# Dealing the products with the values in two stretches per unit

## The chip, the cores and the metric

One core of one Trainium2 chip runs the whole kernel. The metric is the device time of one execution in microseconds (us); the median of three executions of the kernel before is 1018.26 us.

## The reference, cut to what matters

The input `x` has 2048 tokens (rows) of 512 values. A vector `c` gives six modulation rows (shift, scale and gate for each of two blocks). The first block is sliding-window attention with 32 heads of 16 dimensions and a window of 256 tokens, the second a gated feed-forward network with 1792 hidden columns:

```python
mod = (silu(c) @ w_mod).reshape(1, 6, 1, -1)
sa, ca, ga, sb, cb, gb = (mod[:, i] for i in range(6))
h = layernorm(x) * (1 + ca) + sa
q, k, v = split(h @ wqkv)                       # 32 heads of 16
scores = einsum("bhqd,bhkd->bhqk", q, k) / 4
mask = (i_q - i_k >= 0) & (i_q - i_k < 256)
o = softmax(where(mask, scores, -1e9)) @ v
x = x + ga * (o @ wo)
h = layernorm(x) * (1 + cb) + sb
x = x + gb * ((silu(h @ w1) * (h @ w3)) @ w2)
```

With blocks of 128 tokens, a block of queries sees three blocks of keys: its own, the one before and, in part, the one before that. Seen from the keys, a block of keys is needed by up to three blocks of queries.

## The kernel before, in words

The attention is cut into 32 units: 8 groups `g` of four heads by 4 blocks `b` of 512 tokens, unit `u = 4 g + b`. Each unit goes through three stages, and three units are in flight at once:

- **`unit_a(u)`** projects the unit's queries and keys. Twelve products (L412) accumulate in the one PSUM tile `pj`. ScalarE copies the result out three times (L418 `qkr`, L421 `qk0`, L424 `qk1`; in the order qk0, qk1, qkr), GpSimd forms two differences (L430), and six DMAs on SyncE's queue (L435) spread the three parts over the rows of the tile `ring`. These six transfers must have landed before any score of the unit can be computed.
- **`unit_b(u)`** computes 16 score products (L466, tile `mx`, three PSUM tiles in turn), takes the row maxima on VectorE (L473), turns them over (L488) and puts them, by DMA (L497), into four further rows of `ring`.
- **`unit_c(u)`** computes the scores again with the maxima subtracted and the keys on the partitions (L717, tile `st`, three PSUM tiles), masks them in one of three ways (letters C, E, P of `MODE`), and ScalarE writes the exponentials into tiles `pt` (nine of them, in turn). Then come the **products with the values**: `values_of(j, uu)` calls `pv` (L693) for key block `j` of unit `uu`. Each call is four heads, one in each 32-column strip of the PE array, and shows as eight matmul records. All of a unit's products accumulate in one PSUM tile, `po`. When the unit is done, ScalarE copies `po` (L782) and a DMA stores it (L785).

Of key blocks 2 and 3 of a unit, some queries lie in the next 512 tokens. Their products (the "late" ones) are made in the next unit's time, the first of them clearing `po`. They exist for the units with b = 1, 2, 3. In blocks of 128 queries, the products of key blocks 0, 1, 2, 3 of a unit have 3, 3, 2, 1 and the late ones 1 and 2.

The order on every engine is written out by hand. Every operation is given to `at(t, ...)` with a time in ticks; one unit of C is 8 ticks. The list is sorted by `t` and the instructions are issued in that order, so that `t` sets each engine's order and nothing else. A unit of C starts at `8 u`, a unit of A at `8 (u - 3) - 0.975`, a unit of B at `8 (u - 2) + 1.274`. Ticks that matter here, counted from the start of the unit of C that is in flight:

| tick | what |
|---|---|
| 0 to 7.2 | scores of C, two each tick (L717) |
| 1.274, 1.774, ... every 0.5 | scores of B (L466); the first of a new unit at 1.274 |
| 2.377, 4.377, 6.377, 8.377 ... | products with the values, one key block every 2 ticks, four per unit (`X["pv"]` is 4.377) |
| 3.377, 3.477 | the two late products |
| 2.492 | the copy of `po` of the preceding unit |
| 7.025 to 11.227 (that is 3.227 of the next unit) | the twelve products of A (L412), 0.382 apart |

So between the last product of A of a unit (tick 3.227) and the first score of B that needs this unit's rows (tick 9.274) lie, before the change, the late products and those of key blocks 0, 1 and 2; between that score and the next unit's last product of A lies key block 3.

For times past tick 229.9, the operations of attention are put as fixed entries into a list scheduler (`Sched.deal`) that fills the output projection (L1079), the second layernorm and the feed-forward network around them by a model of the engines' times. What it deals in the last three units and after follows from these fixed times too.

Of the kernel before, what the change touches and what calls it, by code (L numbers as in the profile page):

```python
# [28 lines left out]
X = dict(hh=0.184, ra=0.382, ev=(0.407, 0.03, 0.229), mix=(0.805, 0.86), row=(0.832, 0.887, 2.192), tl=0.402, mr=(0.161, 0.359, 1.088), c=(0.363, 1.109, 2.176, 0.003, 0.321, 1.738), pv=4.377, o=(0.115, 0.58), oa=-0.975, ob=1.274)  # L29
# [238 lines left out]
def block_kernel(ctx: ExitStack, tc: tile.TileContext, x, wqk, wv, wo, w13, w2, c, wmod, out):  # L268
# [82 lines left out]
    def queries(rows, a, b, n):  # L351
        return ring[:rows, 1, a, b * P:(b + n) * P]

    def keys(rows, hh, a, b, n):
        return ring[:rows, 2 - 2 * hh, a, b * P:(b + n) * P]
# [291 lines left out]
    def at(t, fn, kind=None):  # L647
        ops.append((t, len(ops), fn, kind))
# [12 lines left out]
    t0 = h0 + 1  # L661
# [27 lines left out]
    def pv(kb, g, pts, qb, c0, nq, first, last):  # L689


        for i in range(4):
            nc.tensor.matmul(po[32 * i:32 * i + DH + 1, qb * P:(qb + nq) * P],  # L693
                             vS[:, kb, 4 * g + i], pts[i // 2][:, i % 2, c0:c0 + nq],
                             start=first, stop=last, skip_group_check=True)

    def unit_c(u, t0, at):

        g, b = divmod(u, NB)
        v = {}  # L700

        def blks(j):
            nq = min(3, NT - 4 * b - j)
            return nq, (2 if nq == 3 else 1), (slice(0, 3, 2) if nq == 3 else slice(0, 1))

        def mode(j, a):
            m = (MODE if u < NU - NL else MODL)[2 * j + a]
            return "D" if m == "C" and NT - 4 * b - j < 3 else m

        def scores(j, a, hh):  # L710
            kb = 4 * b + j
            nq, nm, bl = blks(j)
            if hh == 0:
                held[u, j, a] = a2.tile([P, 2, 3, P], F32, name="pt", bufs=PTB)
            v[j, a, hh] = ps = psA.tile([P, 4, P], F32, name="st", bufs=STB)
            plus = mode(j, a) == "E"
            nc.tensor.matmul(ps[:, :nq], keys(NM, hh, a, kb, 1), queries(NM, a, kb, nq),  # L717
                             start=True, stop=not plus)
            if plus:
                nc.tensor.matmul(ps[:, bl], identr, mskr[:, :nm], start=False, stop=True)  # L720

        def mask(j, a, hh):
            nq, nm, bl = blks(j)
            ps = v[j, a, hh]
            nc.vector.tensor_tensor(out=ps[:, bl], in0=ps[:, bl], in1=mskk[:, :nm], op=ALU.add)

        def probs(j, a, hh):
            nq, nm, bl = blks(j)
            nc.scalar.activation(held[u, j, a][:, hh, :nq], v[j, a, hh][:, :nq], AF.Exp,  # L729
                                 scale=SCALE)  # L730

        def merge(j, a, hh):

            ps = v[j, a, hh]
            nc.vector.copy_predicated(ps[:, 0], later, ps[:, 2])  # L735

        def merged_probs(j, a, hh):
            nc.scalar.activation(held[u, j, a][:, hh, :2], v[j, a, hh][:, :2], AF.Exp, scale=SCALE)  # L738

        def part(j, a):  # L740
            pt = held[u, j, a]
            for m in (1, 0):
                w = dict(WIN[m], fill=0.0)
                w["pattern"] = [[0, 2]] + w["pattern"]
                nc.gpsimd.affine_select(out=pt[:, :, 2 * m], in_=pt[:, :, 0], **w)  # L745

        def side(j, a, hh):
            nq, nm, bl = blks(j)
            ps = v[j, a, hh]
            if hh == 0:  # L750
                v[j, a, "m"] = a2.tile([P, 2, 2, P], F32, name="sm", bufs=1)
            nc.scalar.activation(v[j, a, "m"][:, hh, :nm], ps[:, bl], AF.Copy)
            if nq > 1:
                nc.scalar.activation(held[u, j, a][:, hh, 1], ps[:, 1], AF.Exp, scale=SCALE)

        def side_mask(j, a):
            nq, nm, bl = blks(j)
            sm = v[j, a, "m"]
            for m in range(nm):
                w = dict(WIN[m])  # L760
                w["pattern"] = [[0, 2]] + w["pattern"]
                nc.gpsimd.affine_select(out=sm[:, :, m], in_=sm[:, :, m], **w)

        def side_probs(j, a):
            nq, nm, bl = blks(j)
            nc.scalar.activation(held[u, j, a][:, :, bl], v[j, a, "m"][:, :, :nm], AF.Exp,
                                 scale=SCALE)

        def values_of(j, uu):

            kb = 4 * (uu % NB) + j
            pts = [held[uu, j, a] for a in range(2)]
            nq = min(3, NT - kb)
            here = min(nq, 4 - j)
            if uu == u:
                pv(kb, g, pts, j, 0, here, b == 0 and j == 0, j == 3)
            elif nq > here:
                pv(kb, g, pts, 0, here, nq - here, j == 2, False)

        def out():  # L780
            v["os"] = a2.tile([P, BT], F32, name="os", bufs=1)
            nc.scalar.activation(v["os"], po, AF.Copy)  # L782

        def store():
            nc.sync.dma_start(o_dr[b][g * P:(g + 1) * P, :], v["os"])  # L785

        for j in range(4):
            for a in range(2):
                m, c = mode(j, a), X["c"]
                for hh in range(2):  # L790
                    t = t0 + 2 * j + a + hh * X["hh"]

                    def go(dt, fn, *z):
                        at(t + dt, lambda: fn(*z), fn.__name__)

                    go(0, scores, j, a, hh)
                    if m == "P":
                        go(c[0], side, j, a, hh)
                    elif m == "C":
                        go(c[3], merge, j, a, hh)  # L800
                        go(c[4], merged_probs, j, a, hh)
                    else:
                        if m == "D":
                            go(c[3], mask, j, a, hh)
                        go(c[4], probs, j, a, hh)
                if m == "P":
                    go(c[1], side_mask, j, a)
                    go(c[2], side_probs, j, a)
                elif m == "C":
                    go(c[5], part, j, a)  # L810
            at(t0 + 2 * j + X["pv"], lambda j=j: values_of(j, u), "values")
        if b:
            for j in (2, 3):
                at(t0 + X["pv"] - 1 + (j - 2) * 0.1, lambda j=j: values_of(j, u - 1), "values")
        t1 = t0 + 6 + X["pv"]
        at(t1 + X["o"][0], out, "cut_all")
        at(t1 + X["o"][1], store, "store")
# [60 lines left out]
    for u in range(NU):  # L878
        if u >= 3:
            unit_a(u, 8 * (u - 3) + X["oa"], at)  # L880
        if u >= 2:
            unit_b(u, 8 * (u - 2) + X["ob"], at)
        unit_c(u, 8 * u, at)
        if u % 4 == 2 and u // 4 < 6:
            at(8 * u + 7.65, lambda u=u: gate_load(int(u > 6)))
        if u < len(jobs) and jobs[u]:
            for n, fn in enumerate(jobs[u]):
                at(8 * u + JOB[n], fn)
        if u in (2, 14):
            at(8 * u + 0.3, lambda u=u: copy_raw(u // 14))  # L890
# [674 lines left out]
```

## Time and profile before

| | |
|---|---|
| median of 3 executions | 1018.26 us (1014.97 to 1020.53) |
| profiled execution, its own time | 1016.29 us |
| its span | 1014.6 us |
| mean granted clock of TensorE | 0.993 |
| PE busy | 976.0 us (96%), 5432 matmuls |
| DVE, ACT, POOL busy | 697.9, 562.3, 594.8 us |
| first and last product with the values | 106.7 us, 519.1 us |
| their records | 1408, that is 176 calls of eight |

In the profile PE is TensorE's matmuls and PEld its weight loads, DVE is VectorE, ACT ScalarE, POOL GpSimd, and SP or SPq SyncE with its DMA queue. A matmul's record is longer than what it takes of the engine, because matmuls are pipelined: the time from one start to the next says what it costs. The attention lies between about 94 and 520 us of the span, the output projection and the feed-forward network behind it.

### The profile page before, as it was taken

The numbers are of one execution on the slowest core, as the hardware profiler recorded it, in microseconds if no ns is written. First come the engines' busy times: TensorE is split into PE (matmuls) and PEld (weight loads), VectorE is DVE, ScalarE is ACT, GpSimd is POOL, SyncE is SP. The second block draws the span as 40 slices with busy tenths as digits, with TensorE's granted clock in tenths as the row PEclk, the third lists the DMA queues.
The fourth block names the chain that finished last, engine by engine and source line by source line (L and its number), as shares of the span: only waits on it lengthen the run. The fifth ranks groups of instructions, "written<-read, shape, count | busy, mean of one in ns | idle before, by whom it ended". The sixth has DMA issues, their size and how long they took to land.

```text
span 1014.6 us, 17251 instructions
## 1 busy us (share of the span) xinstructions
PE 976.0 (96%) x5432; PEld 721.6 (71%) x5432; DVE 697.9 (69%) x1878; ACT 562.3 (55%) x1252; POOL 594.8 (59%) x736
## 2 busy tenths in 40 slices
PE   5999999999999999999888899999999999999998
PEld 2578666666666666666456688878888788888886
DVE  7775777777878787878546875566577755665555
ACT  3433777777776777776557766344345444333330
POOL 7341766666665757564548677787786754433420
PEclk9999999999999999999999999999999999999999
DMA  8521353434353434335466066665556343222102
GB/s 296 161 84 43 100 173 125 143 124 144 124 173 123 143 125 148 120 134 173 161 204 221 23 239 195 219 223 193 170 162 194 130 129 93 67 84 66 49 22 83
DMA packets 79983, 141.65 MB, mean 140 GB/s; under 512 B 9234, under 2 KB 22034, under 8 KB 79764
## 3 DMA queue, kind: packets, MB, share of 16 engines
q1 hardware_dynamic: 79172, 139.50, 42.2%
q10 hardware_dynamic: 720, 1.05, 0.3%
q8 instruction: 43, 0.70, 0.3%
q14 instruction: 48, 0.39, 0.1%
HBM read 85.72 MB, written 34.61 MB: 119 GB/s over the span
## 4 chain that ended last, share of the span: by engine, by line
PE 82%; DVE 7%; ACT 4%; DMA 4%; issue 1%; POOL 1%; SPq 0%; POOLq 0%; ACTq 0%; DVEq 0%
PE st L1341 11%; PE mx L1341 11%; PE pj L412 9%; PE mx L466 9%; PE po L693 8%; PE st L717 8%; PE mx L1434 6%; PE st L1434 6%; PE st L631 4%; PE pj L1434 3%; PE pj L1341 3%; PE st L720 1%; PE mx L1079 1%; DMA o_dr<-os 1%; DVE hT L329 1%
## 5 line engine op out<-in xcount | busy, mean ns | idle before, releaser
L473 DVE CUSTOM_DVE_ANT_0 junk<-mx,mskq 128x384 bf16<-128x384 f32 (+2 forms) x512 | 267.5, 528 | 54.2 <-PE mx L466 50.4
L466 PE MATMUL mx<-ring 96*128 96x384 f32 (+2 forms) x512 | 172.9, 351 | 3.9 <-DVE mt L473 2.0
L717 PE MATMUL st<-ring 100*128 100x384 f32 (+2 forms) x512 | 157.1, 343 | 5.7 <-DMA ring<-mT 3.4
L412 PE MATMUL pj<-hT,wq 128*128 128x512 f32 x384 | 153.8, 416 | 1.5 <-DVE hT L329 1.2
L745 POOL TENSOR_SCALAR_AFFINE_SELECT pt<-pt 128x256 f32<-128x256 f32 x224 | 91.4, 413 | 94.5 <-ACT pt L738 86.8
L466 PEld LDWEIGHTS mx<-ring 96*128 96x128 f32 x512 | 94.7, 190 | 61.9 <-DVE mt L473 41.3
L934 POOL TENSOR_TENSOR w<-w,w 128x512 fp32r<-128x512 f32 (+2 forms) x56 | 98.0, 1758 | 56.5 <-ACT w L933 54.2
L738 ACT ACTIVATE pt<-st 128x256 f32<-128x256 f32 x224 | 85.4, 395 | 54.6 <-DVE st L735 53.2
L717 PEld LDWEIGHTS st<-ring 100*128 100x128 f32 x512 | 96.8, 191 | 19.4 <-ACT pt L738 6.6
L693 PE MATMUL po<-pt,vS 128*17 128x384 f32 (+2 forms) x1408 | 108.5, 393 | 0.0
L430 POOL TENSOR_TENSOR qk<-qkr,qk 128x512 fp32r<-128x512 f32 x64 | 82.3, 1286 | 42.6 <-ACT qkr L418 39.4
L729 ACT ACTIVATE pt<-st 128x384 f32<-128x384 f32 (+2 forms) x172 | 77.3, 457 | 37.8 <-PE st L720 32.9
L735 DVE COPY_PREDICATED st<-later,st 128x128 f32<-128x128 uint8 x224 | 65.2, 293 | 46.6 <-PE st L717 46.3
L412 PEld LDWEIGHTS pj<-hT,wq 128*128 128x128 f32 x384 | 72.2, 190 | 26.2 <-issue 17.8
L1372 DVE TENSOR_TENSOR t<-mx,t 128x512 f32<-128x512 f32 x51 | 35.1, 689 | 54.4 <-PE mx L1341 44.5
L1384 POOL TENSOR_TENSOR t<-t,t 128x512 f32<-128x512 f32 x28 | 36.2, 1293 | 58.6 <-DVE t L1372 56.1
L1412 ACT ACTIVATE wq<-g 128x512 fp32r<-128x512 f32 x28 | 17.7, 634 | 92.6 <-DVE g L1368 63.6
L1341 PE MATMUL st<-b,w 128*128 128x512 f32 x264 | 65.9, 392 | 0.6 <-DVE b L1238 0.6
L1372 DVE TENSOR_TENSOR t<-st,t 128x512 f32<-128x512 f32 x50 | 34.3, 688 | 45.8 <-PE st L1341 38.8
L1341 PE MATMUL mx<-b,w 128*128 128x512 f32 x258 | 63.7, 391 | 1.7 <-ACT t L1375 0.9
L1341 PEld LDWEIGHTS mx<-b,w 128*128 128x128 f32 x258 | 48.4, 188 | 12.8 <-ACT t L1375 1.3
L1341 PEld LDWEIGHTS st<-b,w 128*128 128x128 f32 x264 | 49.2, 188 | 11.5 <-DVE b L1238 1.1
(274 smaller groups left out, 2102.4 us busy)
## 6 DMA issues: line engine op xcount, KB each, us to landing
ring<-qk SPq DMA_DIRECT2D x192, 128.0 KB
o_dr<-os SPq DMA_DIRECT2D x32, 256.0 KB
w<-wsum SPq DMA_DIRECT2D x14, 512.0 KB
w<-w2g SPq DMA_DIRECT2D x14, 512.0 KB
jb<-in_w SPq DMA_DIRECT2D x24, 256.0 KB
wraw<-in_w SPq DMA_DIRECT2D x7, 768.0 KB
w<-wraw SPq DMA_DIRECT2D x14, 384.0 KB
vS<-in_wmod SPq DMA_DIRECT2D x20, 256.0 KB
```

The costliest lines, as they stand in the source:

```text
L412: nc.tensor.matmul(v["ps"], WQ[g][w][:, n // 3], hTp(i, n // 3, b * BT, BT), start=(n == 0), stop=(n == 3 * KC - 1))
L430: nc.gpsimd.tensor_tensor(out=v[n], in0=v["raw"], in1=v[1].bitcast(F32), op=ALU.subtract)
L466: nc.tensor.matmul(v[i][:, :n], queries(NS, a, gq, 1), keys(NS, hh, a, k0, gq + 1 - k0), start=True, stop=True)
L473: nc.vector.tensor_tensor_reduce(out=junk[:, :n], in0=v[i][:, :n], in1=mskq[:, 3 * P - n:], scale=1.0, scalar=-3e38, op0=ALU.add, op1=ALU. ...
L693: nc.tensor.matmul(po[32 * i:32 * i + DH + 1, qb * P:(qb + nq) * P], vS[:, kb, 4 * g + i], pts[i // 2][:, i % 2, c0:c0 + nq], start=first, ...
L717: nc.tensor.matmul(ps[:, :nq], keys(NM, hh, a, kb, 1), queries(NM, a, kb, nq), start=True, stop=not plus)
L729: nc.scalar.activation(held[u, j, a][:, hh, :nq], v[j, a, hh][:, :nq], AF.Exp, scale=SCALE)
L738: nc.scalar.activation(held[u, j, a][:, hh, :2], v[j, a, hh][:, :2], AF.Exp, scale=SCALE)
L745: nc.gpsimd.affine_select(out=pt[:, :, 2 * m], in_=pt[:, :, 0], **w)
L934: sch.op(eng, lambda: on_eng(eng).tensor_tensor(out=lo(), in0=src(), in1=hi().bitcast(F32), op=ALU.subtract), 0.06 + 0.0024 * n if eng == ...
L1341: nc.tensor.matmul(ps(bk), WT[s, n][w][:, col], BB[t, k][r], start=start and c == 0, stop=stop and c == 5, skip_group_check=True)
L1434: nc.tensor.matmul(ps(bk), tiles[hk + (h,)][:, i * P:(i + 1) * P], w2_of(last, y, f), start=(m == 0), stop=(m == 5))
```

## The change

The times that the products with the values are given change, and nothing else.

```diff
-            at(t0 + 2 * j + X["pv"], lambda j=j: values_of(j, u), "values")
+            at(t0 + (6 if j else 0) + X["pv"] + 1e-4 * j, lambda j=j: values_of(j, u), "values")
         if b:
             for j in (2, 3):
-                at(t0 + X["pv"] - 1 + (j - 2) * 0.1, lambda j=j: values_of(j, u - 1), "values")
+                at(t0 + X["pv"] + 1e-4 * (j - 4), lambda j=j: values_of(j, u - 1), "values")
```

The preceding unit's two late products are issued directly ahead of key block 0 (tick 4.377 of the unit), and key blocks 1, 2 and 3 directly one behind the other where key block 3 was (tick 10.377, that is 2.377 of the next unit). Key blocks 0 and 3 stay where they were; the late ones move one tick back, key block 1 four ticks and key block 2 two. The number of products, their operands and their tiles stay the same.

## The prediction

> **What bounds the kernel now.** I read the page first: PE is busy 96% of the span, and of the chain that ended last PE has 82%. Then the busy times by stretch, to see whether this holds in the attention, where the change lies:
>
> ```profile
> 100.00:200.00 100.00, 99.25 (x712) 68.45 (x711) 75.99 (x317) 76.31 (x208) 67.26 (x122) 1.00 0.41 134
> 200.00:300.00 100.00, 99.19 (x709) 67.94 (x708) 77.78 (x326) 73.75 (x205) 66.47 (x120) 1.00 0.44 142
> 300.00:400.00 100.00, 99.06 (x719) 66.93 (x718) 78.03 (x323) 74.50 (x207) 66.01 (x116) 1.00 0.42 134
> ```
>
> After the window and its length come PE, PEld, DVE, ACT and POOL, then clock, DMA share and GB/s. PE has no idle time to speak of, at full clock; the others have a quarter free. So PE's own time counts, and I read the timeline of PE alone for what a stretch of products with the values (L693) costs:
>
> ```profile
> 301.59 0.34 PE L466 MATMUL mx<-ring 96*128 96x384 f32 x1
> 301.87 0.84 PE L693 MATMUL po<-pt,vS 128*17 128x384 f32 x8
> 302.63 0.44 PE L466 MATMUL mx<-ring 96*128 96x384 f32 x1
> 302.92 0.28 PE L717 MATMUL st<-ring 100*128 100x256 f32 x1
> ...
> 326.27 0.33 PE L466 MATMUL mx<-ring 96*128 96x384 f32 x1
> 326.53 0.84 PE L693 MATMUL po<-pt,vS 128*17 128x128 f32 x16
> 327.31 0.44 PE L466 MATMUL mx<-ring 96*128 96x384 f32 x1
> 327.59 0.51 PE L717 MATMUL st<-ring 100*128 100x384 f32 x2
> ```
>
> From start to start, a score product of 384 columns takes 0.175 us elsewhere. Ahead of a stretch it takes 0.27, behind it 0.28: 0.10 lost on each side. Inside, 8 records over 128, 256 and 384 columns take 0.34, 0.55 and 0.77: 0.213 for each 128-column block and 0.13 once. The late pair (16 records, three blocks) also takes 0.77, so a second call in the same stretch adds nothing but its blocks. **A stretch costs 0.333 us beside its products**; over all 152 stretches of the trace the median is the same.
>
> Last, I looked for what PE would meet next, and followed one unit from its last projection product (L412) to its first score product (L466):
>
> ```profile
> 352.08 0.40 PE L412 MATMUL pj<-hT,wq 128*128 128x512 f32 x1
> ...
> 353.02 0.63 ACT L421 ACTIVATE qk<-pj 128x512 fp32r<-128x512 f32 x1
> ...
> 353.50 0.72 ACT L424 ACTIVATE qk<-pj,odd 128x512 fp32r<-128x512 f32 x1
> ...
> 353.67 4.96 SPq L435 DMA_DIRECT2D ring<-qk  x6
> ...
> 354.07 0.64 ACT L418 ACTIVATE qkr<-pj 128x512 f32<-128x512 f32 x1
> ...
> 354.79 2.64 POOL L430 TENSOR_TENSOR qk<-qkr,qk 128x512 fp32r<-128x512 f32 x2 [0.97 <-ACT qkr L418]
> ...
> 361.61 0.41 PE L466 MATMUL mx<-ring 96*128 96x384 f32 x1
> ```
>
> This is a chain of latencies that PE covers today. The first copy starts 0.94 after the projection's last start (1.22 where b = 2), the third ends at 2.63, GpSimd's two differences end at 5.35, the last two DMAs are issued at 5.4 and 6.0, and the last lands, by its landing record, mostly 2.3 later: 8.3. A first score follows a landing that it waited for by 0.23 to 0.35 (three units). So it can start no sooner than **8.6 us after the projection's end** (8.9 where b = 2). It starts at 9.5 to 10.05 now: about one us is to spare.
>
> **The sum, part by part.** I cut a period into two windows: the *covered* one, from the projection's last product to the next first score, which the chain runs through, and the *open* one, from there to the next projection's last product. Before, covered and open take 9.55 + 3.25 (b = 0), 10.03 + 2.92 (b = 1), 9.85 + 3.25 (b = 2) and 9.52 + 3.25 us (b = 3), nearly alike in every round.
>
> Removed: b = 0 has 4 stretches and keeps 2, the others have 5 and keep 2, so 8 x 2 + 24 x 3 = 88 of 152 go. Worth 88 x 0.333 = 29.3 us, if PE sets the time everywhere.
>
> Moved: key blocks 1 and 2 of a unit leave the covered window for the stretch at tick 2.377, in the open one. They are 3 + 2 blocks, 5 x 0.213 = 1.07 us. The covered window's PE work falls by that and by two (b = 0) or three stretches: 9.55 - 1.73 = 7.8, 10.03 - 2.07 = 8.0, 9.85 - 2.07 = 7.8, 9.52 - 2.07 = 7.45 us. All lie below the chain's 8.6 or 8.9. PE runs in order, so it must then stand at the first score until the rows land, 0.6 to 1.1 us in every unit. The open window holds one stretch before and after, and grows by the full 1.07: the work is PE's, and DVE and ACT are 2.7 us busy in it.
>
> Can the chain shrink? Its start hangs on events behind the stretch at tick 2.377: PE's scores of tick 3, their four ACT copies, then the projection's copies. I find ACT idle 0.18 us there, waiting for those scores. They come the same time after the stretch as before, so the 0.94 stays. The copy of `po` (L782) waits in ACT's queue for a stretch now 1.07 longer, with the exponentials of ticks 2 and 3 behind it; it finds the same PE order behind the stretch, and I cost it at nothing. If ACT falls behind there, the chain begins later, one for one. The differences on POOL wait for ACT (0.97 in the row above), the DMAs for POOL; nothing else is queued between.
>
> With the typical landing, a period changes by 8.62 - 10.03 + 1.07 = -0.34 (b = 1), 8.95 - 9.85 + 1.07 = +0.17 (b = 2), +0.17 (b = 3), +0.14 (b = 0): +0.14 per round of four, +1 us over 27 steady units. But 6 of these 27 land 0.4 to 1.9 late in the trace (2.7 to 3.9 instead of 2.3, or a late issue) and some others 0.1 or 0.2; today the spare us hides most of it, afterwards nothing does. With every unit's own landing the covered window averages 8.97 against 9.77, and the period changes by +0.27, so 27 x 0.27 = +7.3. The first projection of the steady part lands late already (covered 9.48, wait 0.31): +1.07. I take +6.5, nearer to the upper end, which is what the landings show; +2 to +8.4 are the ends.
>
> Tail, 478 to 520: no projection is left. The stretch at 480 delays a copy of `po` by 1.07 where a chain of DMAs begins; against that, the two units in 500 to 520, PE busy throughout, save five stretches (1.7), and in 494 to 500 PE waits for `ring<-mT` anyway. Together -0.6, but the scheduler deals the output projection and all behind it anew around the moved entries, so 0, from -4 to +4; the feed-forward part after 576 is PE's (310 of 315 us busy), which bounds what another order can do.
>
> Buffers: `pt` has nine tiles. Key block 1's are read later by four ticks, yet the tile's next writer (tick 11.3) waits for scores (tick 11.0) that PE issues behind the stretch at 10.377 anyway. Cost nothing. The later reads also give POOL's masks more time: worth nothing, as no stretch there waits long.
>
> 1016.3 + 6.5 - 0.5 = 1022.3 for an execution like the profiled one; the median of the runs is 2.0 above it: **1024 us**.
>
> **Rivals.** *The saving arrives.* If the chain gives way, PE's 29.3 us come through: 989; by half, if the 0.54 us between the product's end and ACT's first copy vanish, 27 x 0.54 = 15: about 1009. For it: PE is the bound by every view. Against it: the chain is nearly the same to 0.1 us in 27 units, and waits on no PE work once begun. The Trainium skill, TensorEngine Tiling (Array Packing), Key Properties, says that changing the tiling mode drains the engine; the trace agrees that each change costs (0.333 us per stretch), and by that rule alone the change gains the 29.3. Chance 0.15.
>
> *The copying engines fall behind.* In the covered window DVE is busy 7.05 to 7.8 us and ACT up to 7.5, with three `st` and three `mx` tiles between them and PE. I reckon that PE reaches the first score after about 8.4, under the chain. It decides from 8.97 on: if the window stays at 9.5, the loss is (9.5 - 8.97) x 27 = 14 more, 1038; at today's 9.77, 1046. For it: ACT does three projection copies (1.7 us) just when C's exponentials are due. Against: its idle shares. The same page, PSUM Bottleneck, says that tiling speeds up TensorE but not the emptying of PSUM, which may become the limit; the busy shares of 75 to 78% allow it and do not show it. Chance 0.13.
>
> *Nothing merges*, if other entries sort in between: 1018. No other time lies within 0.0003 ticks. Chance 0.02.
>
> **How the numbers follow.** The forecast has 0.70, with its own range from 1015 (typical landings, tail -4) to 1033 (all late landings, tail +4 and some ACT delay). About 0.5%, or 5 us, is what a measurement can tell from no change. Within the forecast, 0.39 lies above 1023.4, 0.29 within, 0.02 below. Slower: 0.39 + 0.13 = 0.52; same: 0.29 + 0.02 + 0.01 of the saving nearly lost = 0.32; faster: 0.02 + 0.14 = 0.16. The range 1011 to 1037 holds the forecast, most of the second rival and little of the first.
>
> **What would show it.** Right: 64 stretches, the long ones 24 records in 1.4 us; a wait for `ring<-qk` of 0.5 to 1 us ahead of the first L466 of nearly every unit, which has one such row before, at 478.6; PE near 95 of 100 us; covered windows near 8.6 to 9, open ones 4.3. Wrong: if the covered window goes below 8.5, the chain was not fixed; if waits for DVE or ACT stand ahead of L466 and L717 instead, the second rival; if attention ends where it did and the time moves, the tail.

## The result and the profile after

| | before | after |
|---|---|---|
| median of 7 executions | 1018.93 us (1014.97 to 1020.53) | 1026.59 us (1023.58 to 1031.15) |
| profiled execution, its span | 1016.29, 1014.6 us | 1026.59, 1024.9 us |
| mean granted clock of TensorE | 0.993 | 0.988 |

The kernel after takes 1.0084 times the time of the kernel before, with a 95% interval of 1.0058 to 1.0110: some 8 us slower. The forecast was 1024, slower.

Where the time lies, from the same marks in both profiled executions (the differences add up to the 10.3 us between them):

| part of the span | before | after | difference |
|---|---|---|---|
| up to the first score of unit 3 | 115.0 | 113.2 | -1.8 |
| 28 units, to the first score of unit 31 (steady part) | 363.6 | 370.6 | +7.0 |
| to the last product with the values | 40.6 | 41.6 | +1.0 |
| to the last product of the output projection | 64.0 | 63.9 | -0.1 |
| first half of the feed-forward products | 201.3 | 203.6 | +2.3 |
| the rest | 230.0 | 232.0 | +2.0 |

Of the -1.8 in the first row, 1.2 us are not of the change: the last product of unit 3's projection starts at 105.5 before and at 104.4 after, ahead of the first product with the values in both kernels, where their orders are the same.

The busy times by stretch, the view that the prediction began with, are now these:

```profile
100.00:200.00 100.00, 96.19 (x702) 68.82 (x701) 74.40 (x315) 74.16 (x205) 66.27 (x122) 1.00 0.40 132
200.00:300.00 100.00, 96.38 (x677) 68.42 (x676) 75.19 (x318) 71.84 (x201) 65.81 (x120) 0.98 0.43 143
300.00:400.00 100.00, 96.68 (x721) 68.32 (x721) 75.66 (x318) 72.65 (x204) 63.30 (x110) 1.00 0.38 126
```

PE was 99.2 busy, and is 96.2 to 96.7: it has about 3 us of idle time in each 100 that it had not, and the other engines have not become busier. The page's chain and two of its groups say the same from two sides, first before, then after:

```profile
PE 82%; DVE 7%; ACT 4%; DMA 4%; issue 1%; POOL 1%; SPq 0%; POOLq 0%; ACTq 0%; DVEq 0%
...
L473 DVE CUSTOM_DVE_ANT_0 junk<-mx,mskq 128x384 bf16<-128x384 f32 (+2 forms) x512 | 267.5, 528 | 54.2 <-PE mx L466 50.4
...
L693 PE MATMUL po<-pt,vS 128*17 128x384 f32 (+2 forms) x1408 | 108.5, 393 | 0.0
```

```profile
PE 70%; DVE 13%; ACT 5%; DMA 4%; issue 4%; POOL 3%; SPq 1%; POOLq 0%; ACTq 0%; DVEq 0%
...
L473 DVE CUSTOM_DVE_ANT_0 junk<-mx,mskq 128x384 bf16<-128x384 f32 (+2 forms) x512 | 262.6, 527 | 88.7 <-PE mx L466 87.8
...
L693 PE MATMUL po<-pt,vS 128*17 128x384 f32 (+2 forms) x1408 | 93.6, 397 | 0.0
```

PE's share of the chain that ended last fell from 82% to 70%. The products with the values are busy 93.6 us instead of 108.5, so the merging took place; and VectorE's maxima (L473) wait 87.8 us for PE's scores instead of 50.4. PE does less, and delivers later.

One unit shows why. This is the timeline from a projection's last product to the next first score of B, the steps that the prediction followed:

```profile
304.48 0.39 PE L412 MATMUL pj<-hT,wq 128*128 128x512 f32 x1
...
305.43 0.63 ACT L421 ACTIVATE qk<-pj 128x512 fp32r<-128x512 f32 x1
...
305.67 1.49 PE L693 MATMUL po<-pt,vS 128*17 128x128 f32 x24
305.90 0.72 ACT L424 ACTIVATE qk<-pj,odd 128x512 fp32r<-128x512 f32 x1
306.08 4.98 SPq L435 DMA_DIRECT2D ring<-qk  x6
306.47 0.64 ACT L418 ACTIVATE qkr<-pj 128x512 f32<-128x512 f32 x1
...
307.19 2.65 POOL L430 TENSOR_TENSOR qk<-qkr,qk 128x512 fp32r<-128x512 f32 x2 [0.97 <-ACT qkr L418]
...
313.07 0.41 PE L466 MATMUL mx<-ring 96*128 96x384 f32 x1 [0.23 <-DVE mt L473]
```

The chain is the old one to the hundredth: first copy 0.95 after the projection's last start (0.94 before), third copy ends at 2.63 (2.63), GpSimd ends at 5.36 (5.35). One stretch of 24 records, 1.42 us from its start to the next product's, stands where three stretches stood. The last of the six DMAs lands at 8.34 by its landing record, and PE's first score starts 0.24 behind it. Before, the same unit's first score came 1.2 us behind the landing. The row names VectorE's `mt` as what ended the wait; the score waits for several things, and an experiment below (e13) shows that the wait moves with the rows. In the 29 units from the first score of unit 3 on, 17 first scores start 0.09 to 0.20 behind the last landing, 11 start 0.24 to 0.46 behind, and one is disturbed.

The periods, in us, as the median over the undisturbed units of each `b` (of the unit of C in flight). "PE ready" is the first score's start less the wait ahead of it, that is, 0.12 behind the start of the product before it, as where there is no wait:

| b | covered window before | PE ready, predicted | PE ready, after | last landing, after | covered window, after | open window, before and after |
|---|---|---|---|---|---|---|
| 0 | 9.55 | 7.8 | 8.22 | 8.36 | 8.56 | 3.25, 4.39 |
| 1 | 10.03 | 8.0 | 8.39 | 8.33 | 8.49 | 2.92, 4.27 |
| 2 | 9.85 | 7.8 | 8.59 | 8.68 | 8.86 | 3.25, 4.38 |
| 3 | 9.52 | 7.45 | 8.20 | 8.34 | 8.48 | 3.25, 4.40 |

The covered window lost 1.0 to 1.5 us, the open one gained 1.1 to 1.35.

The one disturbed unit, in the covered window that begins at 287.4, is worth 3.9 of the 7.0 us. PE's timeline:

```profile
283.37 0.30 PE L466 MATMUL mx<-ring 96*128 96x128 f32 x1 [0.59 <-DMA ring<-qk]
...
289.62 0.77 PE L717 MATMUL st<-ring 100*128 100x384 f32 x2 [1.58 <-DMA ring<-mT]
290.54 2.76 PE L693 MATMUL po<-pt,vS 128*17 128x128 f32 x24
```

and the busy times of the two stretches of 3 us there (after the length: PE, PEld, DVE, ACT, POOL, clock, DMA share, GB/s):

```profile
288.00:291.00 3.00, 1.42 (x16) 1.00 (x19) 1.28 (x7) 2.73 (x9) 2.87 (x5) 0.81 0.45 163
291.00:294.00 3.00, 3.00 (x25) 1.24 (x18) 0.62 (x3) 0.41 (x2) 2.72 (x4) 0.62 0.39 130
```

A landing of the row maxima came late (4.8 us after its issue, where 1.95 is usual in this trace), PE stood 1.58 us for it, and the granted clock was then half for 3.4 us (289.9 to 293.3): the same stretch of 24 records took 2.76 instead of 1.49. Such a stop costs more than its own length.

### The profile page after: what moved, and what is told of

It is laid out like the page before. It is cut to its first block, busy times and chain, and to the rows that moved or that the text cites. A ratio compares the mean times of both kernels' runs of the same rounds, so it can differ in the third digit from the quotient of the medians.

```text
span 1024.9 us, 17239 instructions
## 1 busy us (share of the span) xinstructions
PE 974.1 (95%) x5432; PEld 731.9 (71%) x5432; DVE 687.3 (67%) x1878; ACT 558.4 (54%) x1252; POOL 594.5 (58%) x736
## 3 DMA queue, kind: packets, MB, share of 16 engines
q10 hardware_dynamic: 720, 1.05, 0.3%
## 4 chain that ended last, share of the span: by engine, by line
PE 70%; DVE 13%; ACT 5%; DMA 4%; issue 4%; POOL 3%; SPq 1%; POOLq 0%; ACTq 0%; DVEq 0%
PE mx L1341 11%; PE st L1341 10%; PE po L693 7%; PE mx L1434 7%; PE st L1434 6%; PE mx L466 6%; DVE junk L473 5%; PE pj L412 5%; PE st L717 5%; PE pj L1341 4%; PE st L631 3%; PE pj L1434 2%; POOL qk L430 1%; DMA w<-wraw 1%; DMA ring<-qk 1%
## 5 line engine op out<-in xcount | busy, mean ns | idle before, releaser
L473 DVE CUSTOM_DVE_ANT_0 junk<-mx,mskq 128x384 bf16<-128x384 f32 (+2 forms) x512 | 262.6, 527 | 88.7 <-PE mx L466 87.8
L466 PE MATMUL mx<-ring 96*128 96x384 f32 (+2 forms) x512 | 169.7, 353 | 11.3 <-DVE mt L473 4.7
L717 PE MATMUL st<-ring 100*128 100x384 f32 (+2 forms) x512 | 161.1, 350 | 7.1 <-ACT pt L738 2.5
L412 PE MATMUL pj<-hT,wq 128*128 128x512 f32 x384 | 150.8, 408 | 1.5 <-DVE hT L329 1.2
L693 PE MATMUL po<-pt,vS 128*17 128x384 f32 (+2 forms) x1408 | 93.6, 397 | 0.0
L693 PEld LDWEIGHTS po<-pt,vS 128*17 128x17 f32 x1408 | 35.1, 99 | 41.1 <-issue 26.9
L1341 PE MATMUL st<-b,w 128*128 128x512 f32 x252 | 62.8, 391 | 0.0
L1341 PE MATMUL mx<-b,w 128*128 128x512 f32 x228 | 58.1, 396 | 1.0 <-ACT t L1375 1.0
L1372 DVE TENSOR_TENSOR t<-mx,t 128x512 f32<-128x512 f32 x48 | 32.9, 686 | 34.5 <-PE mx L1341 26.5
L1341 PEld LDWEIGHTS st<-b,w 128*128 128x128 f32 x252 | 47.1, 188 | 10.1
```

The costliest lines, as they stand in the source:

```text
L412: nc.tensor.matmul(v["ps"], WQ[g][w][:, n // 3], hTp(i, n // 3, b * BT, BT), start=(n == 0), stop=(n == 3 * KC - 1))
L466: nc.tensor.matmul(v[i][:, :n], queries(NS, a, gq, 1), keys(NS, hh, a, k0, gq + 1 - k0), start=True, stop=True)
L473: nc.vector.tensor_tensor_reduce(out=junk[:, :n], in0=v[i][:, :n], in1=mskq[:, 3 * P - n:], scale=1.0, scalar=-3e38, op0=ALU.add, op1=ALU. ...
L1341: nc.tensor.matmul(ps(bk), WT[s, n][w][:, col], BB[t, k][r], start=start and c == 0, stop=stop and c == 5, skip_group_check=True)
```

## The experiments

My theory: in the steady units the covered window is set by the chain of latencies from the projection to the rows, so PE's saved stretches turn into waiting, and the products that were moved into the open window are added to the time. Rivals: the copying engines fall behind; the tail and the order that is dealt behind it make the difference; the stretch is not worth its 0.333 us. The medians below stand against the kernel before on the same chip, which took 1016.84 us for e1 to e4, 1017.54 for e5, e6, e7 and e9, and 1016.23 for e11 to e14.

**e1: the change in the steady units alone.** The last units and all that is dealt around them keep the old times.

```diff
-  at(t0 + 2 * j + X["pv"], ...)
+  at(t0 + (((6 if j else 0) + X["pv"] + 1e-4 * j) if u < 27 else (2 * j + X["pv"])), ...)
-  at(t0 + X["pv"] - 1 + (j - 2) * 0.1, ...)
+  at(t0 + ((X["pv"] + 1e-4 * (j - 4)) if u < 28 else (X["pv"] - 1 + (j - 2) * 0.1)), ...)
```

> The new times for the units up to 26 only; from unit 27 on the old ones, so that the last units, and all that the scheduler deals after them, are those of the kernel before. Chain theory (the first score waits for the projection's rows, and key blocks 1 and 2 now lie where nothing covers them): +4 to +7 us, 1023 to 1026. Rival, the loss comes from the last units and from what the scheduler deals anew: no change, within 1 us, or a gain from the stretches saved.

1023.44 us, ratio 1.0063 (1.0044 to 1.0082). The steady part takes 371.3 us, 7.7 more than before (3.8 of it in one unit with the clock halved at 132.7); the two halves of the feed-forward part take 201.3 and 230.0 as before. The steady units by themselves make a loss near the whole one.

**e2: the change in the last units alone**, the same two lines with the conditions turned round.

> The other way about: old times up to unit 26, new times for units 27 to 31. Chain theory: only what the trace shows behind unit 31's first score can move, +1 in the last units and +4.3 in the feed-forward part if its new order is worse: 0 to +5. Rival, all of the loss is here: +8.

1021.12 us, ratio 1.0049 (1.0028 to 1.0070). This is not nothing. Against the profile of before, the part to the last product with the values takes 0.5 more, the output projection 0.3 and the first half of the feed-forward part 2.25; the steady part, unchanged, happened to take 0.8 more. That half took 203.55 here and 203.6 in the kernel after, and 201.1 to 201.3 in before, e1, e3, e4 and e9, which keep the old times in the tail. So the order that is dealt anew around the moved entries costs 2.3 us, long after the last product with the values. e1 and e2 together (+6.6 and +4.3) are more than the whole (+7.7), within the intervals.

**e3: the late products alone**, merged with key block 0 in the steady units; key blocks 1 to 3 keep their times.

```diff
-  at(t0 + X["pv"] - 1 + (j - 2) * 0.1, ...)
+  at(t0 + ((X["pv"] + 1e-4 * (j - 4)) if u < 28 else (X["pv"] - 1 + (j - 2) * 0.1)), ...)
```

> Only the late products are moved, ahead of key block 0 (units up to 27); key blocks 1 and 2 stay where they were. Chain theory: 24 stretches fewer in covered windows that have 0.9 us and more to spare, at 0.333 each: -8 us, 1011. Rival, the cost of a stretch is hidden or only apparent in the records: within 1 us of before.

1017.6 us, ratio 1.0011 (0.9995 to 1.0026): the expected gain of 8 us did not come. The covered windows changed by -0.30 (b = 1), +0.06 (b = 2) and -0.23 (b = 3), where 0.333 was due. For b = 2 the reason is in the timeline, just behind the projection (PE and its weight loads):

```profile
182.53 0.40 PE L466 MATMUL mx<-ring 96*128 96x256 f32 x2
...
182.91 0.81 PE L717 MATMUL st<-ring 100*128 100x384 f32 x2
...
183.28 0.19 PEld L717 LDWEIGHTS st<-ring 100*128 100x128 f32 x1 [0.21 <-ACT pt L754]
...
183.56 0.28 PE L466 MATMUL mx<-ring 96*128 96x256 f32 x1
183.77 0.41 PE L693 MATMUL po<-pt,vS 128*17 128x128 f32 x8
```

From the first of the two `st` products to the score behind them it takes 0.65 us here. Before, it took 0.35, and the late stretch (L693) lay ahead of the two:

```profile
183.30 0.84 PE L693 MATMUL po<-pt,vS 128*17 128x128 f32 x16
...
184.30 0.51 PE L717 MATMUL st<-ring 100*128 100x384 f32 x2
184.65 0.28 PE L466 MATMUL mx<-ring 96*128 96x256 f32 x1
```

That stretch gave ScalarE time; without it PE comes to the second before ScalarE's L754 has emptied its `st` tile, and gives the 0.30 back. A saved stretch is worth 0.333 only where nothing else was about to hold PE. The steady part gained 1.4 us, which the measurement of the whole cannot tell from nothing.

**e4: key blocks 1 and 2 alone**; the late products keep their own stretch.

```diff
-  at(t0 + 2 * j + X["pv"], ...)
+  at(t0 + (((6 if j else 0) + X["pv"] + 1e-4 * j) if u < 27 else (2 * j + X["pv"])), ...)
```

> Only key blocks 1 and 2 are moved into the stretch of key block 3 (units up to 26); the late products keep their own stretch. Chain theory: that stretch lies in the covered window, which then waits for the rows anyway, so the same as e1_steady within 1.5 us. Rival, PE's own work sets the time: 24 x 0.333 = 8 us above e1_steady.

1023.18 us, ratio 1.0061 (1.0037 to 1.0085): what e1 gave, although PE has one stretch more in the covered window of three units in four. The covered windows are 8.4 to 9.0 again. The stretch shows no price, as the theory says, and the 8 us of the rival are refuted. A smaller price is not: by e3's covered windows the stretch is worth some 3 us in all, which the intervals of e1 and e4 cannot tell from nothing. That the two are alike also says that the loss comes from key blocks 1 and 2, and not from the late products. No unit here met a halved clock, and the steady part is 369.2: 5.6 us more than before.

**e9: only key block 2 moved**, key block 1 left on its own: half of the work goes into the open window.

```diff
-  at(t0 + 2 * j + X["pv"], ...)
+  at(t0 + (((0, 2, 6, 6)[j] + X["pv"] + 1e-4 * j) if u < 27 else (2 * j + X["pv"])), ...)
```

The late products are merged as in e1.

> Three stretches: the late products with key block 0, key block 1 alone at its old place, key block 2 with key block 3 (units up to 26). Only 2 blocks, 0.43 us, go into the open window instead of 1.07, and the covered window keeps about 8.4 to 8.9 us of work. Chain theory: -0.33 (b = 0), -0.67, -0.47, -0.47 us per unit, about -13 in all, less what is lost to waits for ACT as in e3_late (about 4): 1007 to 1010. Rival, moving any block into the open window costs more than a stretch saves: 1018 or more.

1016.7 us, ratio 1.0000 (0.9979 to 1.0022): no gain either, and the expectation missed. PE is ready at 8.79, 8.97, 9.17 and 8.54 (b = 0 to 3), which is 0.76, 1.06, 0.68 and 0.99 less than before, where two blocks and one or two stretches make 0.76 and 1.09: all of it arrives except for b = 2, as in e3. But the open window grew by 0.6 (0.76 for b = 1) and not by 0.43, and units whose rows land late now wait for them. By the medians, the periods fall by some 0.6 in a round of four, about 4 us over the steady part; 1.4 were left in the profiled execution.

**e5: take the wait for the rows away**, by starting B one tick later, with the order of e1.

```diff
-  unit_b(u, 8 * (u - 2) + X["ob"], at)
+  unit_b(u, 8 * (u - 2) + X["ob"] + (1.0 if u < 30 else 0.0), at)
```

> e1_steady, with all of unit B one tick later (units up to 29), so that the first score lies at tick 2.274 and the products between 1.274 and 2.274 move from the open window into the covered one. Chain theory: the covered window then has more work than the chain is long (7.8 + 1.4 = 9.2 us against 8.6), nobody waits for the rows, and the saving of the stretches comes through: 0.7 to 0.9 us per unit over 27 units, some 998 to 1003 us (20 to 25 below e1_steady). Rival, the engines that empty PSUM have become the limit: 1018 or more, with waits for DVE and ACT ahead of L466 and L717. What e3_late showed (a stretch taken away gave 0.16 of the 0.33 us, as a score product then waited for ACT instead) says that a part is lost: 1003 to 1010.

1040.82 us, ratio 1.0230 (1.0213 to 1.0248). The rows land 0.7 to 4.7 us ahead of the first score, so that wait is gone, but another is there. The waits of PE in the attention:

```profile
PE st L717 <- DMA ring<-mT: 29.1, 19, 2.1
PE st L717 <- ACT qkr L418: 2.4, 1, 2.4
```

(us in total, times, longest.) The scores of C read the rows of the maxima (`mT`), which the end of B writes; moved by a tick, they come too late for them. The units that do not meet this wait (b = 3) have a period of 12.46 us, against 12.76 before and some 12.85 after: by these units, the new order can be faster where no landing ends last. The experiment shows the new wait, and does not by itself prove the old one.

**e6 and e7: shorten the chain.** The first difference goes to VectorE, which takes 0.7 us where GpSimd takes 1.3; e6 with the order of e1, e7 with that of before.

```diff
-  nc.gpsimd.tensor_tensor(out=v[n], in0=v["raw"], in1=v[1].bitcast(F32), op=ALU.subtract)
+  (nc.vector if n == 1 else nc.gpsimd).tensor_tensor(out=v[n], in0=v["raw"], ...)
```

> e1_steady, with the first of the two differences of the projection (L430) on VectorE instead of GpSimd, so that both are made at once and the last rows are issued 0.7 us sooner. The order on PE is that of e1_steady. Chain theory: the covered window ends 0.6 us sooner, at about 8.0, where PE's own work or ACT ends it: -0.5 x 27 = -13 us against e1_steady, 1009 to 1013. Rival, the engines that empty PSUM set the window: less than 3 us below e1_steady.

> The same difference on VectorE in the kernel before, all else as there. Chain theory: the chain has 1 us to spare in most units, so a shorter one brings only what late landings cost now: 0 to -2 us, 1015 to 1017. Rival, the chain sets the time in both kernels: -10 or more. VectorE's extra 27 x 0.69 us lie in its idle quarter.

e6: 1033.58 us, ratio 1.0157 (1.0137 to 1.0176). e7: 1035.06 us, ratio 1.0171 (1.0154 to 1.0188). In e6 the rows land 0.6 us earlier, at 7.75, as expected, and yet PE comes to its first score at 8.76 in nearly every unit, a full us behind the rows. The new difference heads VectorE's queue until ScalarE's third copy is done, with the maxima queued behind it and PE's scores waiting for their tiles. So the pair is confounded: VectorE is loaded in both. What can be read is that with the rows out of the way the new order is no slower than the old, 1033.6 against 1035.1.

**e11 and e12: start the chain earlier.** The projection comes 0.93 ticks earlier and the copy of `po` later, behind the projection's three copies; e11 with the order of e1, e12 with that of before.

```diff
-  at(t1 + X["o"][0], out, "cut_all")
-  at(t1 + X["o"][1], store, "store")
+  at(t1 + (0.75 if u < 27 else X["o"][0]), out, "cut_all")
+  at(t1 + (1.3 if u < 27 else X["o"][1]), store, "store")
...
-  unit_a(u, 8 * (u - 3) + X["oa"], at)
+  unit_a(u, 8 * (u - 3) + X["oa"] - (0.93 if 3 < u < 31 else 0.0), at)
```

> e1_steady, with unit A 0.93 ticks earlier (units 4 to 30), so that the projection ends at tick 2.30, just ahead of the stretch at 2.377, and the copy of po put behind the projection's copies in ACT's order. The whole stretch then lies in the covered window; unit B and its rows of maxima stay where they were (what e5_first_score lost). Chain theory: the covered window has some 10 us of work against a chain of 8.6, the open one falls to about 2 us, and the stretches saved come through: about 12.3 us per unit, 0.5 to 0.7 less than before, 1002 to 1009. Rival, with PE faster the engines that empty PSUM set the time: 1014 or more, with no wait for the rows of ring.

> The same earlier projection and later copy of po in the kernel before, with its five stretches. Chain theory: the chain has an us to spare there already and gains more, PE's own work stays the same: within 3 us of before, a little less if late landings no longer cost anything, 1013 to 1019. Rival, the earlier projection by itself is what helps in e11_early_pj_after: 8 us or more below before.

e11: 1041.83 us, ratio 1.0253 (1.0230 to 1.0275). e12: 1112.3 us, ratio 1.0935 (1.0904 to 1.0967). The rows are 1.4 to 2.8 us ahead of the first score in e11, and PE waits for other engines instead:

```profile
PE mx L488 <- DVE mr L482: 19.4, 25, 1.1
PE st L717 <- ACT pt L754: 18.6, 26, 0.9
```

In e12 the late products meet the later copy of `po`, a wait that the merged order does not have (`PE po L693 <- ACT os L782`, 28.2 us), and the clock is granted at 0.88 to 0.91 between 100 and 400 us. The old order depends on where the copies of ScalarE lie, so the pair compares more than one thing and settles nothing about the rows. It does show what stands next: with the landing out of the way, PE stands for VectorE's preparation of the row maxima (L482) and for ScalarE's emptying of the score tiles (L754). The Trainium skill, TensorEngine Tiling (Array Packing), PSUM Bottleneck, says that tiling speeds up TensorE and not the emptying of PSUM, which may then be the limit; the row for `pt` in e11 agrees, 18.6 us of waiting for a tile to be emptied, though no run here leaves the tiling out.

**e13 and e14: lengthen the chain.** One more operation on GpSimd ahead of the second difference; its result is not used. e13 with the order of e1, e14 with that of before. If the rows end last in the new order and not in the old, the same addition must cost its length in one and nothing in the other.

```diff
+  if 2 < u < 31:
+      nc.gpsimd.tensor_tensor(out=spare, in0=ident, in1=o32, op=ALU.subtract)
   nc.gpsimd.tensor_tensor(out=v[n], in0=v["raw"], ...)
```

> e1_steady, with one more GpSimd operation of 128 x 128 (some 0.46 us, it writes a tile that nobody reads) between the two differences of the projection, units 3 to 30: the last rows are issued 0.46 us later, nothing else changes. Chain theory: the chain sets every unit's time, so + 0.46 x 27 = +12 against e1_steady, 1033 to 1037. Rival, something else ends the covered window: less than 4 above e1_steady.

> The same added operation in the kernel before. Chain theory: 1 us is to spare in most units and takes it, late landings cost 0.4 more in a quarter of them: +1 to +4. Rival, the added operation costs its time wherever it stands (GpSimd or its masks are the limit): the same +12 as in e13_longer_after.

e13: 1028.12 us, ratio 1.0133 (1.0110 to 1.0155). e14: 1016.52 us, ratio 1.0002 (0.9988 to 1.0017). The second difference started 0.30 us later, not the 0.46 that the operation's own record shows and that the expectation went by: the records overlap by 0.04 at each end, and 0.08 lay idle between the two differences without it. So the chain's price is 27 x 0.30 = 8.1 us. The new order pays 7 us of it (1.0133 against e1's 1.0063; 4 to 10 by the two intervals), the old one 0.2 (-1.2 to 1.7). In e13 PE is ready when it was, at 8.2 to 8.6, the rows land 0.3 later (8.64 instead of 8.33), the median wait ahead of the first score rises from 0.25 (after) to 0.56, and the gaps between landing and first score keep their values. That is how a wait named `DVE mt` is known to be one for the rows. The busy times of the same stretch in the two kernels:

```profile
200.00:300.00 100.00, 94.23 (x693) 67.26 (x693) 74.64 (x315) 71.92 (x201) 68.45 (x126) 1.00 0.43 137
```

```profile
200.00:300.00 100.00, 99.22 (x709) 68.08 (x709) 77.60 (x326) 73.83 (x205) 69.06 (x128) 1.00 0.44 142
```

PE is busy 94.2 in e13, the first of them, against 96.4 after the change; in e14 it is 99.2, as before. This pair changes the chain and no instruction of PE, ScalarE or VectorE, and it decides between the theory and the rival: in the new order the landing of the rows ends last.

No version was faster than the kernel before; e3, e9 and e14 equal it.

## Why the prediction was right

**Right:** a stretch still takes 0.33 us beside its products, 64 stretches are left, the chain from the projection kept its times, and the moved products stand in the open window with 1.13 us where 1.07 was reckoned (1.35 for b = 1). The steady part lost what was forecast, 6.5: by the medians e1 loses 6.6 and e4 6.3, and in the profiled execution it went from 363.6 to 370.6, +7.0.

**In part luck:** 3.9 of these 7.0 us are the one unit with the halved clock, for which the sum has no term. All other units make +3.1 (+3.9 in e1, which has such a unit too, and +5.6 in e4, which has none). Typical units changed by +0.05 to +0.2 (b = 0), -0.2 (b = 1), +0.1 (b = 2) and +0.1 (b = 3), close to the forecast's +0.14, -0.34, +0.17 and +0.17, and alone make about 1 us. That leaves some 2 us for late landings of the rows in this trace, where the forecast took 5.5.

**Right sum, wrong inside:** the step "the covered window's PE work falls to 7.45 to 8.0". PE is ready only at 8.2 to 8.6. It took the stretches as if nothing else held PE between them. In e3 ScalarE did; in the kernel after it is VectorE, in the unit shown above, where key block 1's stretch stood before:

```profile
308.36 0.92 PE L466 MATMUL mx<-ring 96*128 96x384 f32 x2
...
308.83 0.19 PEld L466 LDWEIGHTS mx<-ring 96*128 96x128 f32 x1 [0.34 <-DVE mt L473]
...
309.11 0.22 PE L717 MATMUL st<-ring 100*128 100x128 f32 x1
```

Two scores take 0.75 us from start to start, where 0.35 is usual, because the second waits for a tile that VectorE's maxima free: 0.40 us, more than the 0.333 that the stretch there had cost. So PE stands 0.25 us at the first score by the median, and not 0.6 to 1.1; the mark "a wait of 0.5 to 1 us in nearly every unit, named `ring<-qk`" failed in size and in name. The time came out right because the landing sets it in most units in any case; the prediction's own remark under the second rival, that PE reaches the score after about 8.4, was the better number. It matters for the saving: with the landing free, 26 units would gain 0.36 us each (the mean wait), about 9 us, and the kernel would stand about where it stood before, not 29 us below (an estimate, which no run shows).

**The landing's last step** was taken as 0.3; it is 0.13 in most units. Hence covered windows of 8.42 to 8.5, which the text would have read as a chain that was not fixed. The chain was fixed; only this term was too large. The unit that the prediction shows, at 352.08, is a late one: its rows land at 9.23, 0.3 ahead of its first score.

**The tail** is the term that was mis-sized in earnest: its paragraph puts it at 0, from -4 to +4, and the sum has -0.5. e2 measures +4.3 by the medians, 2.8 to 7.1 by its interval, of which 2.3 is the feed-forward part's new order. PE fills that part, as the forecast says (its 310 of 315 us are those from 700 on; from 583 on PE is busy 427 of 431), which bounds what a new order can gain and says nothing on what it can lose. The 2.6 us between the forecast and the median are less than this term was off.

**The rivals.** The saving did not arrive, since the chain did not give way. The copying engines did not fall behind as far as the point given for them (8.97), but waits for them, like the two shown in e3 and above, keep PE at 8.2 to 8.6, a quarter of a us ahead of the rows. The two limits lie that close, which fits that no experiment that freed one of them won. Two things stay open: how much of the one unit with the halved clock belongs to the change (e1 and the kernel after have one each, e4 and the kernel before none in the steady part), and the last 2.0 us, behind the middle of the feed-forward products, of which e2 shows 0.2. There PE waits 2.29 us for VectorE at 806.8 in the profiled execution of the kernel after.

## What to carry to other kernels

An engine that is busy 99% has work under which latencies hide. Before its work is cut or moved, follow the longest chain that it covers from the same event and compare the two ends: here 1.2 us were to spare, and the change was to take 1.7 to 2.1 us of PE's work out of the covered window and took 1.3 to 1.6, 1.1 of it only moved into the open one: the saving became a wait and the move a loss. To show which of two near limits ends last, lengthen one by a known bit in both versions: 0.30 us on the chain cost 7 us in one order and nothing in the other, while the attempts to shorten it each brought a new wait.

## What the runs showed of the hardware

The granted clock was halved for stretches of 3.4 us, or two or three of them in a row (6.8; 10.2 in e11 and e12), also after waits of PE that were much shorter than such a stretch: in the kernel after at 289.9, behind the wait of 1.58 us and with PE busy 1.42 of the 3 us from 288 to 291; in e1 at 132.7, behind 1.40 us; in the kernel before at 479.9, behind 1.51 us. A wait of 1.30 us in the kernel after, at 166, was not followed by one. Products at the halved clock took nearly twice their time (2.76 us instead of 1.49 for 24 records), so a wait of 1.6 us in a unit made that unit 3.9 longer.

A small operation of VectorE was held up beside one of GpSimd. The two rows, from the kernel after:

```profile
299.62 1.26 POOL L835 TENSOR_TENSOR jb<-jb,wqr 128x512 f32<-128x512 f32 x1
299.72 1.20 DVE L482 SCALAR_TENSOR_TENSOR mr<-mt,mr 128x16 fp32r<-128x16 f32 x1
```

L482 takes 0.215 us by the mean over 26 of them, and 1.20 here, ending 0.04 behind GpSimd's. The Trainium skill, SBUF — State Buffer, Who interferes with whom, states that VectorE and GpSimd share one pair of ports, which one of them holds for a whole instruction, and that a VectorE instruction with two inputs in SBUF contends with a GpSimd instruction that reads SBUF. Both rows read two tiles in SBUF, and their ends agree with it; no run here separates the two. PE waited 1.05 us for this at 300.97.
